# Left-over keys' scores of two pairs as quadrant products, with one tanh and one exp for both

## The chip, the cores and the metric

One core of one Trainium2 chip. The metric is the device time of one execution in microseconds (us), the median of several runs. The instructions of five engines appear below: TensorE (PE; its weight loads are PEld), VectorE (DVE), ScalarE (ACT), GpSimd (POOL) and SyncE (SP), which only starts transfers here. Each engine works through its own queue in order.

## The reference

Attention with a soft cap over 8 batches of 12 heads, 448 positions and 64 dimensions, then a channel mix over the 768 columns of all heads:

```python
scores = scale * q @ k.T                    # per head, 448 x 448
scores = cap * tanh(scores / cap)
attn = exp(scores - max); attn /= attn.sum(-1) + 1e-9
x = attn @ v                                # heads side by side: [8, 448, 768]
x_prev = x shifted by one position
xk = mu_k * x + (1 - mu_k) * x_prev         # xr with mu_r likewise
k = relu(xk @ w_k);  v2 = (k * k) @ w_v     # 768 -> 1024 -> 768
out = sigmoid(xr @ w_r) * v2
```

All tensors are float32.

## The kernel before, in words

The 96 heads are 48 pairs. A program of 55 steps runs pair i's scores, tanh and exp in step i, the values' product of pair i-1, the normalisation and mixing of pair i-2, and the cutting of queries and keys of pair i+2. From step 7 on the products of the key weights (xk @ w_k) of the batch that is complete are spread over the steps as well (`kpart`, line 388: 24 products of 448 columns a step, in four parts K). The products with w_v and w_r fill the second half of the program, from about 547 us on, and the change doesn't touch them.

Scores are computed transposed, keys on the partitions. A pair's 448 keys are three groups of 128 (g = 0, 1, 2) and 64 left-over keys (g = 3). Precision comes from cutting each float32 operand into a high and a low part of a faster type and adding three products (high by high, low by high, high by low). The cutting is `qk_high` (line 180) and `qk_low` (line 202), on GpSimd for most pairs, over tiles of 960 columns: 448 queries, 384 keys, and 128 columns in which the left-over keys of the two heads stand beside zeros, so that one product over all 128 rows gives the scores of both heads (`scores`, line 231; its products are line 238).

`tanh` (line 243, the instruction at 246) and `exp` (line 249, instruction at 256) work on both heads' scores of a group, 128x896, or on 128x448 for g = 3. `red` (line 282, instruction at 284) sums exponentials on VectorE; `gather` (288), `recip` (292), `rec_store` and `rec_load` carry the sums through memory and bring back their reciprocals. `values` (line 258) multiplies uncut float32: line 267 for the groups, and line 277 for the left-over keys of an even and the following odd pair together, in the step behind the odd pair (from pair 6 on; before that, for each pair by itself). In line 277 each product uses 64 rows and 64 columns of the array, one of its four quadrants.

`norm` (line 316, instruction at 317) scales the values' sums; `mix_old` (ScalarE, 327) writes over their accumulator; `mix_new` (VectorE, 332) reads it and releases it. The accumulators `pv` have two buffers, the scores' accumulators `s` have two buffers of two banks. `x_high` and `x_low` (GpSimd, helper lines 93 and 103) cut xk. `gate_old` (GpSimd, 350) and `gate_new` (VectorE, 344) mix for the gate, from pair 12 on.

The order of every queue is written out by hand, as strings of operations that `step` (line 734) walks through. `STEP` serves steps 14 and on (`STEP_2` every sixth of them), `STEP_6` steps 7 to 13, `STEP_7` step 6, `STEP_0` steps 0 to 5. In them S0 to S3 are the scores of the groups, V the values' product, K a part of the key weights' products, and each f one of five VectorE operations that rebuild float32 from the float64 weights (`weight_round`, line 461; in steps up to 42). GpSimd adds their result at line 491 (`weight_sum`). Each engine takes its operations in the order in which they stand there.

Of the kernel before, what the change touches and what calls it, by code (L numbers as in the profile page):

```python
# [13 lines left out]
ALU = mybir.AluOpType  # L14
# [29 lines left out]
KM = 3 * P  # L44
KC = KM + P
LAG = 7
# [20 lines left out]
STEP_6 = """gather load_v x_store weight_load weight_low S0 S1 V S2 f f f f f tanh0 exp0 red0 norm  # L67
weight_sum tanh1 exp1 K relu_early red1 tanh2 qk_rise relu exp2 mix_old k_store mix_new recip rec_store qk_low x_high x_low gate_old
K red2 weight_rest weight_sum relu k_store S3 K K weight_abs tanh3 exp3 red3 gate_new relu k_store load_qk rec_load weight_store"""
STEP_7 = """gather rec_load load_v x_store weight_load weight_low S0 S1 V0 S2 V1 S3 V2 V3 f f f f f tanh0 exp0 red0  # L70
# [8 lines left out]
class Body:  # L79
# [82 lines left out]
    def init_attn(self):  # L162
        self.raw, self.QK, self.rawv, self.S, self.P32, self.PV, self.R, self.rs = ({} for _ in range(8))
        self.tails, self.stored = [], []
# [20 lines left out]
    def qk_first(self):  # L185

        raw = self.raw.pop(0)
# [14 lines left out]
    def qk_low(self, i, e="p"):  # L202
        hi, = self.QK[i]
        lo = self.qp.tile([P, S + KC], F32R, name="qkl")
        self.sub(e, lo, self.raw.pop(i), f(hi))
        self.QK[i] = (hi, lo)

    def row_maxima(self, i):
# [3 lines left out]
        for h in range(2):  # L212
            t = HALF[h]
            for c in range(4):
# [3 lines left out]
                for k, w in ((slice(0, KM), KM), (slice(KM, S), 64)):  # L218
                    first = S + (KM + 64 * ((h + i) % 2) if w == 64 else 0)
# [6 lines left out]
        nc.sync.dma_start(self.max_d.rearrange("h (c p) -> p (h c)", c=4), m)  # L226
        self.M = self.rawp.tile([P, 2, S], F32, name="M", bufs=1)
        for h in range(2):
            nc.sync.dma_start(self.M[:, h], self.max_d[h:h + 1, :].to_broadcast([P, S]))

    def scores(self, i, g):
        nc, qk = self.nc, self.QK[i]
        s = self.ps_s.tile([P, 2, 512], F32, name="s")
        k = slice(S + g * P, S + (g + 1) * P)

        for n, (a, b) in enumerate(((0, 0), (1, 0), (0, 1))):
            for h, p in enumerate(HALF) if g < 3 else [(0, slice(0, P))]:
                nc.tensor.matmul(s[:, (h + i) % 2 if g < 3 else 0, 0:S], qk[a][p, k], qk[b][p, 0:S], start=(n == 0), stop=(n == 2))  # L238
        if g == 3:
            self.QK.pop(i)  # L240
        self.S[i, g] = s

    def tanh(self, i, g):
        n = 2 if g < 3 else 1
        p32 = self.p32p.tile([P, n, S], F32, name=f"p32_{n}", bufs=5 if g < 3 else 3)
        self.nc.scalar.activation(p32, self.S.pop((i, g))[:, :n, 0:S], AF.Tanh, scale=self.scl_t)  # L246
        self.P32[i, g] = p32

    def exp(self, i, g):
        p32 = self.P32[i, g]  # L250
        if self.maxima:
            for h in range(2):
                p, c = (slice(0, P), (h + i) % 2) if g < 3 else (HALF[(h + i) % 2], 0)
                self.nc.vector.scalar_tensor_tensor(out=p32[p, c, :], in0=p32[p, c, :], scalar=self.cap_t[p],
                                                    in1=self.M[p, h, :], op0=ALU.mult, op1=ALU.subtract)
        self.nc.scalar.activation(p32, p32, AF.Exp, scale=1.0 if self.maxima else self.cap_t)  # L256

    def values(self, i, part=None):
# [475 lines left out]
    def step(self, i, KS):  # L734

        nk = nq = 0
        if self.maxima and i < NPAIR:
            self.row_maxima(i)
# [4 lines left out]
        for op in (STEP_0 if i < 6 else STEP_7 if i == 6 else STEP_6 if i < REST[0] else STEP_2 if i % NP == 2 else STEP).split():  # L743
            j = pair.get(op)
# [180 lines left out]
def _layout(inputs):  # L925
# [5 lines left out]
    kt = inputs["k"].reshape(B, NP, 2, S, D).swapaxes(3, 4)  # L931
    qk[..., S:S + KM] = kt[..., :KM]
    v[..., :3, :, :] = vp[:, :, :, :KM].reshape(B, NP, 2, 3, 2, 64, D).transpose(0, 1, 4, 5, 3, 2, 6)
    for h in range(2):
        for odd in range(2):
            t = (h + odd) % 2
            qk[:, odd::2, h, :, S + KM + 64 * t:S + KM + 64 * t + 64] = kt[:, odd::2, h, :, KM:]
            v[:, odd::2, t, :, 3, h] = vp[:, odd::2, h, KM:]
# [26 lines left out]
```

## Time and profile before

| | us |
|---|---|
| median of 3 runs | 913.62 |
| lowest and highest | 912.69, 914.09 |
| span of the profiled execution | 910.9 |
| profiled execution's own time | not listed apart; the runs above lie 1.8 to 3.2 above the span |
| TensorE busy | 889.0 (98%) |
| VectorE, ScalarE, GpSimd busy | 710.2, 642.4, 401.5 |

The profile is one execution, recorded by the hardware. The span runs from the first to the last instruction. An engine's busy time counts its instructions but not their waits. TensorE's matmuls overlap, so one lasts longer than the distance to the next; the cost of one is the distance between starts. A float32 product that isn't cut shows as two instructions, so the values' products of three groups and two heads are "x12". In the chain of waits each piece is the time from its start to the start of the next piece.

### The profile page before, as it was taken

Reading aid. Unit: us, or ns where it says so; the run is one execution under the profiler, and the core shown is the slowest. Engines: PE = TensorE matmul, PEld = TensorE weight load, DVE = VectorE, ACT = ScalarE, POOL = GpSimd, SP = SyncE. Lnnn points to the kernel's source line nnn. Section 1 sums busy time; section 2 is a strip of 40 time slices with the busy share of each in tenths; the row PEclk is TensorE's granted clock in tenths of the full one; section 3 lists DMA queues with packets and bytes.
Section 4 is the critical chain, followed back from the end, with each engine's and each line's share of the span. In section 5 each row is a group of like instructions: output and inputs, shape, how many; then the busy total and the mean of one; then the engine's idle time right before and its main releaser. Section 6 shows DMA issues by size and latency. Waiting matters only on the chain.

```text
span 910.9 us, 15135 instructions
## 1 busy us (share of the span) xinstructions
PE 889.0 (98%) x4986; PEld 713.7 (78%) x4986; DVE 710.2 (78%) x1246; ACT 642.4 (71%) x950; POOL 401.5 (44%) x342
## 2 busy tenths in 40 slices
PE   7879999999999999999999999999999999999996
PEld 3336666667766666766666789999999999999996
DVE  6989976888887888888867766778878767777775
ACT  8998888888878888888877575566565535555553
POOL 5996554777666666776664200000000014444330
PEclk8999999999999999999999999999999999999999
DMA  5565555666666656666565465745454546677663
GB/s 174 163 214 197 187 166 186 203 210 186 208 201 208 204 187 207 206 199 205 163 223 170 128 237 159 240 156 176 143 162 154 180 141 189 217 219 221 215 219 111
DMA packets 123673, 171.61 MB, mean 188 GB/s; under 512 B 22592, under 2 KB 107712, under 8 KB 123584
## 3 DMA queue, kind: packets, MB, share of 16 engines
q1 hardware_dynamic: 114224, 155.67, 54.7%
q10 hardware_dynamic: 9360, 14.88, 4.4%
q8 instruction: 41, 0.67, 0.3%
q14 instruction: 48, 0.39, 0.2%
HBM read 111.48 MB, written 56.60 MB: 185 GB/s over the span
## 4 chain that ended last, share of the span: by engine, by line
PE 87%; DMA 4%; DVE 3%; ACT 2%; SPq 2%; issue 1%; ACTq 0%; DVEq 0%
PE ps L609 39%; PE kps L406 23%; PE s L238 12%; PE pv L267 11%; DMA r<-rec_d 2%; PE pv L277 2%; DMA rec_d<-rs 1%; SPq L290 1%; DVE r L284 1%; ACT p L246 1%; DVE x L317 1%; SPq L313 1%; ACT wvh L724 1%; ACT p L256 0%; DVE xk L332 0%
## 5 line engine op out<-in xcount | busy, mean ns | idle before, releaser
L284 DVE TRANSPOSE_TENSOR_REDUCE r<-p 128x28 f32<-128x896 f32 x192 | 183.5, 979 | 20.1 <-ACT p L256 18.8
L246 ACT ACTIVATE p<-s,scl_t 128x896 f32<-128x896 f32 x192 | 173.2, 902 | 27.8 <-PE s L238 23.9
L256 ACT ACTIVATE p<-p,cap_t 128x896 f32<-128x896 f32 x192 | 182.1, 948 | 6.0 <-ACT pv L327 1.2
L406 PE MATMUL kps<-xkh,wkh 128*128 128x448 f32 x372 | 140.5, 378 | 0.5 <-ACT ko L413 0.5
L406 PE MATMUL kps<-xkl,wkh 128*128 128x448 f32 x372 | 136.0, 365 | 0.0
L406 PE MATMUL kps<-xkh,wkl 128*128 128x448 f32 x372 | 135.9, 365 | 0.0
L573 POOL TENSOR_TENSOR s<-src 128x384 f32<-128x384 f32 x14 | 14.3, 1021 | 265.0 <-DVE lo L594 265.0
L267 PE MATMUL pv<-p,rv 128*64 128x448 f32 x576 | 124.6, 561 | 6.6 <-DVE xk L332 6.6
L609 PE MATMUL ps<-wvh,hi 128*128 128x384 f32 x392 | 131.0, 334 | 0.0
L609 PE MATMUL ps<-wvl,hi 128*128 128x384 f32 x392 | 131.0, 334 | 0.0
L593 ACT CAST hi<-s 128x512 fp32r<-128x512 f32 (+1 forms) x112 | 63.6, 568 | 89.3 <-PE ps L609 76.9
L594 DVE TENSOR_TENSOR lo<-s,hi 128x512 fp32r<-128x512 f32 (+1 forms) x112 | 70.8, 632 | 58.8 <-ACT hi L593 43.7
L103 POOL TENSOR_TENSOR qkl<-rqk,qkh 128x960 fp32r<-128x960 f32 x47 | 106.8, 2273 | 9.9 <-ACT qkh L97 6.6
L609 PE MATMUL ps<-wrh,hi 128*128 128x384 f32 x294 | 98.6, 335 | 0.3 <-DVE o L632 0.3
L609 PE MATMUL ps<-wrl,hi 128*128 128x384 f32 x294 | 98.5, 335 | 0.0
L491 POOL TENSOR_TENSOR wsq<-wa,wsq 128x384 f32<-128x384 f32 (+1 forms) x40 | 44.0, 1100 | 110.7 <-DVE wsq L484 77.1
L593 ACT CAST hi<-src 128x512 fp32r<-128x512 f32 (+1 forms) x84 | 47.6, 567 | 62.3 <-PE ps L609 59.4
L238 PE MATMUL s<-qkh 64*128 64x448 f32 (+1 forms) x336 | 83.5, 439 | 7.8 <-ACT qkh L97 4.1
L238 PEld LDWEIGHTS s<-qkh 64*128 64x128 f32 (+1 forms) x336 | 36.8, 188 | 68.7 <-issue 27.5
L267 PEld LDWEIGHTS pv<-p,rv 128*64 128x64 f32 x576 | 36.4, 138 | 65.3 <-issue 56.2
L406 PEld LDWEIGHTS kps<-xkh,wkh 128*128 128x128 f32 x372 | 69.8, 188 | 20.3 <-issue 13.8
L609 PE MATMUL ps<-wvh,lo 128*128 128x384 f32 x392 | 83.7, 334 | 0.0
(109 smaller groups left out, 1812.8 us busy)
## 6 DMA issues: line engine op xcount, KB each, us to landing
rqk<-qk SPq DMA_DIRECT2D x47, 480.0 KB
k_d<-ko ACTq DMA_DIRECT2D x64, 224.0 KB
src<-k_d SPq DMA_DIRECT2D x56, 256.0 KB
rv<-v SPq DMA_DIRECT2D x48, 256.0 KB
r<-rec_d SPq DMA_DIRECT2D x96, 112.0 KB
v_d<-o SPq DMA_DIRECT2D x56, 192.0 KB
src<-x_d SPq DMA_DIRECT2D x42, 256.0 KB
vl<-v_d SPq DMA_DIRECT2D x56, 192.0 KB
```

The source lines that it names most:

```text
L103: {"p": self.nc.gpsimd, "v": self.nc.vector}[e].tensor_sub(*a)
L238: nc.tensor.matmul(s[:, (h + i) % 2 if g < 3 else 0, 0:S], qk[a][p, k], qk[b][p, 0:S], start=(n == 0), stop=(n == 2))
L246: self.nc.scalar.activation(p32, self.S.pop((i, g))[:, :n, 0:S], AF.Tanh, scale=self.scl_t)
L256: self.nc.scalar.activation(p32, p32, AF.Exp, scale=1.0 if self.maxima else self.cap_t)
L267: nc.tensor.matmul(pv[p, 0:S], v[:, g, h, :], ph[:, (h + i) % 2, :], start=(g == 0), stop=False)
L277: nc.tensor.matmul(self.PV[j][p, 0:S], v[t, 3, h, :], ph[t, 0, :], start=False, stop=True)
L284: self.nc.vector.tensor_reduce(out=r1[:, 0:RM].rearrange("p (x g) -> p x g", g=3)[:, :, g] if g < 3 else r1[:, RM:RC], in_=p32.rearrange(" ...
L406: nc.tensor.matmul(self.kps[fc][:, 0:S], w, m[:, dc, :], start=first, stop=last)
L491: {"p": self.nc.gpsimd, "v": self.nc.vector}[e].tensor_add(sq, f(a), sq)
L593: self.nc.scalar.copy(hi, x)
L594: self.nc.vector.tensor_sub(lo, x, f(hi))
L609: self.nc.tensor.matmul(o, a[:, c, :], w[:, c, :], start=first and k == 0, stop=last and k == len(todo) - 1, skip_group_check=True)
```

## The change

The left-over keys are no longer cut or packed beside zeros: a pair's tile has 896 columns (448 queries, 448 keys). Their scores are computed for an even pair and the following odd one together, in the even pair's step, from the raw float32 tiles: four products, one for each pair and head, each in one quadrant of the array, into the two banks of one `s` tile. In steps 8 and on S3 stands directly behind V, whose last products are quadrants too in even steps. One tanh and one exp over 128x896 serve both pairs. The sums stay separate: `red3` of an odd pair runs at the head of its own step, behind the five weight operations. The raw tiles live longer, so they have three buffers instead of two. The step strings become pairs, for even and odd steps. The scratch size for transfers started by GpSimd, of which there are none, goes to 256. The branch for `maxima` does not run with this input.

```diff
-KC = KM + P
+KC = S
...
-STEP = """gather load_v quad_load x_store weight_load S0 S1 V S2 f f f f f tanh0 exp0 red0
+ODD = """gather load_v quad_load x_store weight_load S0 S1 V S2 f f f f f red3 tanh0 exp0 red0
 weight_sum tanh1 exp1 red1 norm recip rec_store K qk_high qk_low tanh2 relu mix_old k_store prep mix_new x_high x_low gate_old
-K exp2 red2 weight_rest weight_sum relu k_store prep S3 K prep K tanh3 exp3 red3 gate_new relu k_store prep
+K exp2 red2 weight_rest weight_sum relu k_store prep K prep K gate_new relu k_store prep
 weight_abs load_qk rec_load quad_load tail_open weight_store"""
-STEP_2 = STEP.replace("K qk_high", "K S3 qk_high").replace("prep S3 K", "prep K")
-STEP_0 = """gather rec_load load_v x_store weight_load S0 S1 V0 S2 V1 S3 V2 V3 f f f f f tanh0 exp0 red0
-weight_sum tanh1 exp1 weight_abs red1 recip rec_store qk_high qk_low tanh2 exp2 norm red2 tanh3 exp3 mix_old red3 mix_new x_high x_low
+EVEN = ODD.replace("V S2", "V S3 S2").replace(" red3", "").replace("tanh2", "tanh3 tanh2").replace("K gate_new", "K exp3 red3 gate_new")
+ODD_0 = """gather rec_load load_v x_store weight_load S0 S1 V0 S2 V1 V2 V3 f f f f f red3 tanh0 exp0 red0
+weight_sum tanh1 exp1 weight_abs red1 recip rec_store qk_high qk_low tanh2 exp2 norm red2 mix_old mix_new x_high x_low
 load_qk weight_store"""
+EVEN_0 = ODD_0.replace("V1", "V1 S3").replace(" red3", "").replace("red2", "red2 tanh3 exp3").replace("mix_new", "red3 mix_new")
...
     def load_qk(self, i):
-        t = self.raw[i] = self.rawp.tile([P, S + KC], F32, name="rqk")
+        t = self.raw[i] = self.rawp.tile([P, S + KC], F32, name="rqk", bufs=3)
...
     def scores(self, i, g):
-        nc, qk = self.nc, self.QK[i]
-        s = self.ps_s.tile([P, 2, 512], F32, name="s")
+        nc = self.nc
+        s = self.S[i, g] = self.ps_s.tile([P, 2, 512], F32, name="s")
+        if g == 3:
+            for j in (i, i + 1):
+                raw = self.raw.pop(j)
+                for h, p in enumerate(HALF):
+                    nc.tensor.matmul(s[HALF[(h + j) % 2], j % 2, 0:S], raw[p, S + KM:S + KC], raw[p, 0:S], start=True, stop=True)
+            return
+        qk = self.QK[i]
...
     def tanh(self, i, g):
-        n = 2 if g < 3 else 1
-        p32 = self.p32p.tile([P, n, S], F32, name=f"p32_{n}", bufs=5 if g < 3 else 3)
-        self.nc.scalar.activation(p32, self.S.pop((i, g))[:, :n, 0:S], AF.Tanh, scale=self.scl_t)
-        self.P32[i, g] = p32
+        p32 = self.p32p.tile([P, 2, S], F32, name="p32" if g < 3 else "p3", bufs=5 if g < 3 else 2)
+        self.nc.scalar.activation(p32, self.S.pop((i, g))[:, :, 0:S], AF.Tanh, scale=self.scl_t)
+        self.P32[i, g] = p32
+        if g == 3:
+            self.P32[i + 1, g] = p32
...
-                    nc.tensor.matmul(self.PV[j][p, 0:S], v[t, 3, h, :], ph[t, 0, :], start=False, stop=True)
+                    nc.tensor.matmul(self.PV[j][p, 0:S], v[t, 3, h, :], ph[t, j % 2, :], start=False, stop=True)
...
         p32, r1 = self.P32[i, g], self.r1[i % 2]
+        if g == 3:
+            p32 = p32[:, i % 2:i % 2 + 1]
...
-    nc = _bacc.Bacc("TRN2", target_bir_lowering=False, num_devices=1)
+    nc = _bacc.Bacc("TRN2", target_bir_lowering=False, num_devices=1, dynamic_dma_scratch_size=256)
```

`STEP_6` becomes `ODD_6` and `EVEN_6` in the same way: red3 of the odd step behind its f's, S3 behind V in the even step, tanh3 ahead of tanh2, exp3 and red3 behind weight_abs.

## Rows read from the trace of the kernel before

**Rows 1.** Busy time by engine in two windows: window, length, each engine, granted clock, DMA share, GB/s

```profile
28.00:38.00 10.00, 8.24 (x37) 3.01 (x37) 9.12 (x18) 9.80 (x13) 9.44 (x9) 0.83 0.58 176
112.00:505.00 393.00, 393.00 (x2226) 269.44 (x2227) 313.31 (x553) 322.75 (x410) 254.82 (x209) 1.00 0.62 196
```

**Rows 2.** Chain of waits, 155 to 180 us, one early and one late piece: start, length, what

```profile
by line: PE kps L406 41.0%; PE pv L267 28.9%; PE s L238 28.2%; PE pv L277 3.7%
...
155.83 2.41 PE pv L267 x12
...
161.70 0.61 PE s L238 x3
...
166.19 2.41 PE pv L267 x12
168.60 0.91 PE pv L277 x8
...
177.46 2.41 PE pv L267 x12
...
20.37 0.90 PE pv L277 x4
...
457.72 2.41 PE pv L267 x12
```

**Rows 3.** VectorE in order of time: start, length, operation, idle before and releaser

```profile
152.18 0.63 DVE L332 SCALAR_TENSOR_TENSOR xk<-x,mu_k,pv 128x448 f32<-128x448 f32 x1
...
305.49 0.65 DVE L284 TRANSPOSE_TENSOR_REDUCE r<-p 128x14 f32<-128x448 f32 x1 [0.89 <-ACT p L256]
306.90 0.69 DVE L344 SCALAR_TENSOR_TENSOR xg<-x,mu_r,xg 128x448 f32<-128x448 f32 x1 [0.77 <-POOL xg L350]
...
309.75 2.10 DVE L284 TRANSPOSE_TENSOR_REDUCE r<-p 128x28 f32<-128x896 f32 x2
...
313.67 0.63 DVE L332 SCALAR_TENSOR_TENSOR xk<-x,mu_k,pv 128x448 f32<-128x448 f32 x1
...
317.63 0.69 DVE L344 SCALAR_TENSOR_TENSOR xg<-x,mu_r,xg 128x448 f32<-128x448 f32 x1 [1.73 <-POOL xg L350]
```

**Rows 4.** GpSimd in order of time, the same step

```profile
311.98 2.27 POOL L103 TENSOR_TENSOR qkl<-rqk,qkh 128x960 fp32r<-128x960 f32 x1
314.39 0.57 POOL L93 TENSOR_SCALAR xkh<-xk 128x448 fp32r<-128x448 f32 x1
...
316.18 1.42 POOL L350 TENSOR_SCALAR xg<-x,om_r 128x448 f32<-128x448 f32 x1
```

**Rows 5.** TensorE in order of time, after two early idle times

```profile
31.36 1.18 PE L267 MATMUL pv<-p,rv 128*64 128x448 f32 x4 [1.30 <-DVE xk L332]
...
35.52 0.47 PE L238 MATMUL s<-qkh 128*128 128x448 f32 x1
...
40.30 0.97 PE L267 MATMUL pv<-p,rv 128*64 128x448 f32 x4 [0.69 <-DVE xk L332]
...
42.91 0.47 PE L238 MATMUL s<-qkh 128*128 128x448 f32 x1
```

**Rows 6.** Groups by line and shape: exp and tanh on ScalarE

```profile
L256 ACT ACTIVATE p<-p,cap_t 128x896 f32<-128x896 f32 x144 | 149.9, 1041 | 4.5 <-ACT pv L327 1.2
L246 ACT ACTIVATE p<-s,scl_t 128x896 f32<-128x896 f32 x144 | 143.5, 997 | 25.3 <-PE s L238 23.9 <-ACT ko L413 0.8
...
L256 ACT ACTIVATE p<-p,cap_t 128x448 f32<-128x448 f32 x48 | 32.2, 671 | 1.6
...
L246 ACT ACTIVATE p<-s,scl_t 128x448 f32<-128x448 f32 x48 | 29.6, 618 | 2.4 <-ACT ko L413 2.4
```

**Rows 7.** Waits from 111 to 505 us: total, times, longest

```profile
ACT pv L327 <- DVE x L317: 24.5, 27, 1.9
```

**Rows 8.** Chain of waits before 110 us, two pieces

```profile
12.00 0.53 ACT p L246
...
39.08 0.60 DVE r L284
```

More of the change, by code (lines that the diff above doesn't have):

```diff
@@ L52 @@
 LATE = [*range(12), NPAIR - 2, NPAIR - 1]
-STEP = """gather load_v quad_load x_store weight_load S0 S1 V S2 f f f f f tanh0 exp0 red0
+ODD = """gather load_v quad_load x_store weight_load S0 S1 V S2 f f f f f red3 tanh0 exp0 red0
 weight_sum tanh1 exp1 red1 norm recip rec_store K qk_high qk_low tanh2 relu mix_old k_store prep mix_new x_high x_low gate_old
-K exp2 red2 weight_rest weight_sum relu k_store prep S3 K prep K tanh3 exp3 red3 gate_new relu k_store prep
+K exp2 red2 weight_rest weight_sum relu k_store prep K prep K gate_new relu k_store prep
 weight_abs load_qk rec_load quad_load tail_open weight_store"""
-STEP_2 = STEP.replace("K qk_high", "K S3 qk_high").replace("prep S3 K", "prep K")
-STEP_0 = """gather rec_load load_v x_store weight_load S0 S1 V0 S2 V1 S3 V2 V3 f f f f f tanh0 exp0 red0
-weight_sum tanh1 exp1 weight_abs red1 recip rec_store qk_high qk_low tanh2 exp2 norm red2 tanh3 exp3 mix_old red3 mix_new x_high x_low
+EVEN = ODD.replace("V S2", "V S3 S2").replace(" red3", "").replace("tanh2", "tanh3 tanh2").replace("K gate_new", "K exp3 red3 gate_new")
+ODD_0 = """gather rec_load load_v x_store weight_load S0 S1 V0 S2 V1 V2 V3 f f f f f red3 tanh0 exp0 red0
+weight_sum tanh1 exp1 weight_abs red1 recip rec_store qk_high qk_low tanh2 exp2 norm red2 mix_old mix_new x_high x_low
 load_qk weight_store"""
-STEP_6 = """gather load_v x_store weight_load weight_low S0 S1 V S2 f f f f f tanh0 exp0 red0 norm
+EVEN_0 = ODD_0.replace("V1", "V1 S3").replace(" red3", "").replace("red2", "red2 tanh3 exp3").replace("mix_new", "red3 mix_new")
+ODD_6 = """gather load_v x_store weight_load weight_low S0 S1 V S2 f f f f f red3 tanh0 exp0 red0 norm
 weight_sum tanh1 exp1 K relu_early red1 tanh2 qk_rise relu exp2 mix_old k_store mix_new recip rec_store qk_low x_high x_low gate_old
-K red2 weight_rest weight_sum relu k_store S3 K K weight_abs tanh3 exp3 red3 gate_new relu k_store load_qk rec_load weight_store"""
+K red2 weight_rest weight_sum relu k_store K K weight_abs gate_new relu k_store load_qk rec_load weight_store"""
+EVEN_6 = ODD_6.replace("V S2", "V S3 S2").replace(" red3", "").replace("tanh2", "tanh3 tanh2").replace("weight_abs", "weight_abs exp3 red3")
 STEP_7 = """gather rec_load load_v x_store weight_load weight_low S0 S1 V0 S2 V1 S3 V2 V3 f f f f f tanh0 exp0 red0
@@ L162, in init_attn @@
     def init_attn(self):
-        self.raw, self.QK, self.rawv, self.S, self.P32, self.PV, self.R, self.rs = ({} for _ in range(8))
+        self.raw, self.QK, self.rawv, self.S, self.P32, self.PV, self.R, self.rs, self.M = ({} for _ in range(9))
         self.tails, self.stored = [], []
     def load_qk(self, i):
-        t = self.raw[i] = self.rawp.tile([P, S + KC], F32, name="rqk")
+        t = self.raw[i] = self.rawp.tile([P, S + KC], F32, name="rqk", bufs=3)
         self.load_part(i, slice(0, S + (KC if i else P)))
@@ L185, in qk_first @@
     def qk_first(self):
-        raw = self.raw.pop(0)
+        raw = self.raw[0]
         hi, lo = self.QK[0] = [self.qp.tile([P, S + KC], F32R, name=n) for n in ("qkh", "qkl")]
@@ L204, in qk_low @@
         lo = self.qp.tile([P, S + KC], F32R, name="qkl")
-        self.sub(e, lo, self.raw.pop(i), f(hi))
+        self.sub(e, lo, self.raw[i], f(hi))
         self.QK[i] = (hi, lo)
@@ L218, in row_maxima @@
                 for k, w in ((slice(0, KM), KM), (slice(KM, S), 64)):
-                    first = S + (KM + 64 * ((h + i) % 2) if w == 64 else 0)
+                    first = S + k.start
                     for n, (a, b) in enumerate(((0, 0), (1, 0), (0, 1))):
@@ L251, in exp @@
         if self.maxima:
-            for h in range(2):
-                p, c = (slice(0, P), (h + i) % 2) if g < 3 else (HALF[(h + i) % 2], 0)
+            for j, h in [(i, 0), (i, 1)] + [(i + 1, 0), (i + 1, 1)] * (g == 3):
+                p, c = (slice(0, P), (h + i) % 2) if g < 3 else (HALF[(h + j) % 2], j % 2)
                 self.nc.vector.scalar_tensor_tensor(out=p32[p, c, :], in0=p32[p, c, :], scalar=self.cap_t[p],
-                                                    in1=self.M[p, h, :], op0=ALU.mult, op1=ALU.subtract)
+                                                    in1=self.M[j][p, h, :], op0=ALU.mult, op1=ALU.subtract)
         self.nc.scalar.activation(p32, p32, AF.Exp, scale=1.0 if self.maxima else self.cap_t)
@@ L736, in step @@
         nk = nq = 0
-        if self.maxima and i < NPAIR:
-            self.row_maxima(i)
+        if self.maxima and i < NPAIR and i % 2 == 0:
+            for j in (i, i + 1):
+                self.row_maxima(j)
         pair = dict(load_qk=i + 3, qk_high=i + 2, qk_low=i + 2, qk_rise=i + 2, load_v=i, S=i, tanh=i, exp=i, red=i)
@@ L742, in step @@
         pair["x_store"] = i - 3
-        for op in (STEP_0 if i < 6 else STEP_7 if i == 6 else STEP_6 if i < REST[0] else STEP_2 if i % NP == 2 else STEP).split():
+        for op in ((EVEN_0, ODD_0) if i < 6 else (STEP_7,) if i == 6 else (EVEN_6, ODD_6) if i < REST[0] else (EVEN, ODD))[i % 2].split():
             j = pair.get(op)
@@ L931, in _layout @@
     kt = inputs["k"].reshape(B, NP, 2, S, D).swapaxes(3, 4)
-    qk[..., S:S + KM] = kt[..., :KM]
+    qk[..., S:] = kt
     v[..., :3, :, :] = vp[:, :, :, :KM].reshape(B, NP, 2, 3, 2, 64, D).transpose(0, 1, 4, 5, 3, 2, 6)
@@ L936, in _layout @@
             t = (h + odd) % 2
-            qk[:, odd::2, h, :, S + KM + 64 * t:S + KM + 64 * t + 64] = kt[:, odd::2, h, :, KM:]
             v[:, odd::2, t, :, 3, h] = vp[:, odd::2, h, KM:]
```

14 lines of the change are left out of this document (7 added, 7 removed).

## The prediction, made before the change was built

> **What bounds the kernel now.** I read the windows first, then the chain of waits, then each engine's order in time. From 112 to 505 us, most of the attention stage, TensorE is busy in every microsecond while VectorE, ScalarE and GpSimd are busy for 313, 323 and 255 of the 393 us [rows 1]. The chain of waits agrees: from 155 to 180 us it never leaves TensorE [rows 2]. So a step there costs the sum of its products. The values' first product starts at 155.83 in step 15 and at 457.72 in step 43; that is 301.9 us for 28 steps, 21.56 for two. The odd step shown takes 10.36 and the even one 11.27, on average a little less, because the last keys' value products of two pairs stand in the even one (0.91, against 0.61 for the scores of one pair's left-over keys) [rows 2].
>
> A share of 80% says little about a queue that runs in order, so I looked for a loop in VectorE's and GpSimd's orders. There is one. gate_new starts at 306.90 and 317.63, 10.73 apart, and nothing in between waits for TensorE [rows 3]: gate_new and the five weight operations take 2.85 (to 309.75), red0, red1, norm and recip 3.92 (to 313.67), mix_new and the hand-over 0.72, GpSimd's x_high, x_low and gate_old 3.24 (from 314.39) [rows 3, 4]. GpSimd isn't what binds there: qk_low ends at 314.25, mix_new at 314.30, x_high starts at 314.39 [rows 3, 4]. This loop of 10.73 a step stands beside TensorE's 10.78. The small reduction red3 costs nothing in it today: it runs at 305.49, after VectorE has waited 0.89 for it, and 0.77 of waiting for GpSimd follows [rows 3].
>
> The loop reaches TensorE through V, the values' product: its accumulator has two buffers, and V of a step needs mix_new of the step before. Early on V waits for exactly that (1.30 at 31.36) [rows 5]. At step 15 mix_new ended at 152.81, 3.0 us ahead of V [rows 2, 3].
>
> **The change, part by part.**
>
> *Scores of the left-over keys.* Two steps lose 2 x 0.61 = 1.22 [rows 2]. They gain four quadrant products. Their price isn't in the trace; the nearest rows are the values' quadrant products, 0.91 for two pairs with a change of array layout ahead, and a third of the 2.41 that three layers of uncut float32 products take, 0.80 [rows 2]. The new ones follow products of their own layout, so I take 0.80 and keep 0.91 as the other end. TensorE saves 0.42 in two steps, 0.21 a step: 21.14 for two, an odd step 9.7, an even one 11.4.
>
> Do the four really run side by side? One pair's value quadrants (two row halves of the array, one accumulator bank) take 0.90 and two pairs' take 0.91 [rows 2], so neither the halves nor the pairs wait for each other. The Trainium skill (TensorEngine Tiling (Array Packing), "Gotcha 1: PSUM Pressure") says that different row tiles cannot access one PSUM bank at the same time. Here each pair's two halves write one bank, so by that rule the new scores would take 1.6, not 0.80; the trace speaks against it with the 0.90.
>
> *One tanh and exp for two pairs.* ScalarE drops 2 x (0.618 + 0.671) and gains 0.997 + 1.041: 0.54 less in two steps, but 0.75 more in the even one [rows 6]. From 112 us on that is off the path. tanh3 now stands ahead of tanh2, so mix_old, queued behind, comes up to 1.0 later; it waits for norm by 0.9 on average anyway (24.5 us in 27 waits) [rows 7]. Were ScalarE late all the same, mix_new would come later by as much, at most the 1.0. exp3 no longer has tanh3 just ahead of it, so the even step's red3 isn't later than now.
>
> *red3 of odd pairs.* It moves from the slack ahead of gate_new to the place behind the five weight operations, ahead of red0. There it is inside the loop: red0, red1, norm, recip and mix_new queue behind it, then GpSimd, then gate_new. It never waits (its data is a step old) but it costs its length: 0.65 alone, half of a large one (2.10 / 2 / 2 = 0.53) at least [rows 3]. I take 0.55. The loop becomes 10.73 in even steps and 11.28 in odd ones: 22.0 for two, against TensorE's new 21.14.
>
> *Cuts.* 64 of 960 columns leave qk_high and qk_low: some 0.15 off 2.27 [rows 4], hidden, since x_high waits for mix_new; each load of queries and keys shrinks by the same 64 columns, and nothing on the path waits for one. The third buffer for raw keys, the second accumulator of the row maxima's branch and the DMA scratch size move no instruction that runs here; SP's order is unchanged. SP's gather for odd pairs can go after red2.
>
> **The sum**, against the profiled span of 910.9 (its own total isn't listed; the three runs lie 1.8 to 3.2 above the span, the median 2.7, and I keep that distance).
> - Steps 0 to 6: the chain goes through ScalarE in step 0 (tanh3 at 12.00), later norm, red2, red3, gather, the sums' load, norm again [rows 8]. Odd steps lose red3 from it (0.60, steps 3 and 5), the first two steps 0.54 of ScalarE: -1.75. If ScalarE's heavier even step takes its place: 0; with a shorter wait ahead of red2: -2.5.
> - 68 to 112 us: chains through several engines; 0, give or take 1.
> - 112 to 155: four steps at -0.21: -0.85.
> - Steps 15 to 42: TensorE alone would save 28 x 0.21 = 5.9. Its lead of 3.0 falls by 0.86 in two steps: V of step 16 has 1.45 left (3.0 + 9.7 - 11.28), step 18 0.6, step 20 waits 0.25, and the eleven even steps 22 to 42 wait 0.86 each, 9.7 in all. Net +3.8.
> - Steps 43 to 47: no weight operations, the loop is over 2 us shorter and catches up: -1.05. Behind that: 0.
>
> Together -1.75 - 0.85 + 3.8 - 1.05 = +0.15: 913.8 us, no difference that this kernel's measurement (about 0.2%, 1.8 us) can tell.
>
> The new waits of 0.86 could lower TensorE's clock. From 28 to 38 us the granted clock is 0.83 on average, so part of it was at 1.2 GHz and not at 2.4 [rows 1]: after an idle 1.30 there the next products took 4.16 (31.36 to 35.52), while after an idle 0.69 the same products took 2.61 (40.30 to 42.91) [rows 5]. A fall would cost 1.55 in one step, but the loop doesn't wait for TensorE, so the waits behind it would shrink by as much; under 1 us would remain.
>
> **The rivals.**
> *TensorE stays the bound.* Then every step from 112 to 505 saves 0.21: 36.5 x 0.21 = 7.7, with 1.75 early 9.4: 904.4 us. It needs room in the loop that I don't see: a VectorE wait between the weight operations and mix_new into which red3 falls. For it: the lead of 3.0 is never used up today. Against: at 309.75 the reductions follow the weight operations with no wait [rows 3].
> *The row halves wait for each other* (slower). The change then doesn't do what it says: the new scores take 1.6 on TensorE in each even step, more than the 1.22 they replace. Two steps take 21.94, the loop's 22.0 hardly binds, and 0.38 more for each two of 36.5 steps is +6.9; less 1.75: 918.8 us. It decides from about 1.3 us for four products. The 0.90 of one pair's quadrants speaks against it; for it, only that scores and values differ in their source.
>
> **How the numbers follow.** The loop case gets 0.62, TensorE as the bound 0.25, serial halves 0.13. Inside the loop case the early gain (0 to -2.5), red3's length (0.53 to 0.65, eleven times), the quadrants' 0.80 to 0.91 and 68 to 112 us give 911 to 917.5; I split it 0.18 faster, 0.26 the same, 0.18 slower by over 0.2%. With the rivals: faster 0.43, same 0.26, slower 0.31. The range reaches down past the first rival, 903.5, and up to 917.5; it leaves out the second.
>
> **What the new profile would show.** Right: in the even steps from about 20 to 42, V waits 0.8 to 0.9 for mix_new (some 10 us in all); gate_new's spacing alternates between 10.7 and 11.3; the four new products take 0.8. Wrong: no such waits and 21.1 for two steps (the first rival), or 1.6 for the products (the second). Also wrong: gate_new still 10.7 apart after odd steps, or VectorE waiting ahead of red0 for exp0.

## The result and the profile after

The changed kernel takes 919.71 us (median of 4 runs, 917.79 to 923.07) against 913.15 us (912.53 to 914.09) beside it: 1.0078 times the time before, 95% interval 1.0056 to 1.0101. It is slower by some 6 us. The forecast was 913.8, with a range that ended at 917.5.

The profiled execution has a span of 920.9 us, 10.0 more than before; with 923.07 it is the slowest of the four, so the split below shows some 3 us more than the medians do. The marks of the split stand in both traces: the values' first product in steps 15 and 43, norm of step 48 (the last but one), the first product of the stage that follows the attention, and the end of the span. Differences are taken before rounding.

| from, to | before | after | difference | forecast |
|---|---|---|---|---|
| start, values of step 15 | 155.8 | 158.0 | +2.1 | -2.6 |
| step 15, step 43 | 301.9 | 304.7 | +2.8 | +3.8 |
| step 43, norm of step 48 | 57.8 | 58.2 | +0.5 | -1.05 |
| norm of 48, next stage | 31.4 | 34.5 | +3.1 | 0 |
| next stage, end | 364.0 | 365.5 | +1.5 | 0 |

The loop in the 28 steps in the middle came out as the forecast's theory had it. First VectorE in the order of time (start, length, operation, idle before it and releaser), one odd and one even step, to be held against [rows 3]:

```profile
307.78 0.63 DVE L343 SCALAR_TENSOR_TENSOR xk<-x,mu_k,pv 128x448 f32<-128x448 f32 x1
...
311.72 0.69 DVE L355 SCALAR_TENSOR_TENSOR xg<-x,mu_r,xg 128x448 f32<-128x448 f32 x1 [1.04 <-POOL xg L361]
...
314.57 2.63 DVE L295 TRANSPOSE_TENSOR_REDUCE r<-p 128x14 f32<-128x448 f32 x3
...
319.01 0.62 DVE L343 SCALAR_TENSOR_TENSOR xk<-x,mu_k,pv 128x448 f32<-128x448 f32 x1
...
322.95 0.68 DVE L355 SCALAR_TENSOR_TENSOR xg<-x,mu_r,xg 128x448 f32<-128x448 f32 x1 [2.29 <-POOL xg L361]
```

gate_new (line 355) to gate_new is 11.23 us here, 10.73 in [rows 3]; the next spacing is 10.71 again, and so in turn. The three reductions red3, red0, red1 take 2.63, where two took 2.10: red3 costs 0.53 in the loop. GpSimd, in the same step, now waits for VectorE where it had work up to that point in [rows 4]:

```profile
319.72 0.57 POOL L95 TENSOR_SCALAR xkh<-xk 128x448 fp32r<-128x448 f32 x1 [0.84 <-DVE xk L343]
...
321.51 1.41 POOL L361 TENSOR_SCALAR xg<-x,om_r 128x448 f32<-128x448 f32 x1
```

And TensorE waits for mix_new in the even step, then runs the values' products (276, 286) and the four new score products (240):

```profile
319.69 2.48 PE L276 MATMUL pv<-p,rv 128*64 128x448 f32 x12 [0.63 <-DVE xk L343]
322.09 0.98 PE L286 MATMUL pv<-p,rv 64*64 64x448 f32 x8
322.90 0.93 PE L240 MATMUL s<-rqk 64*64 64x448 f32 x8
323.76 0.47 PE L247 MATMUL s<-qkh 64*128 64x448 f32 x2
```

The eight instructions of the four score products start in two groups of four, the four of a group within 0.02 us and the groups 0.38 apart (322.90 to 322.92, 323.27 to 323.29), so the four run side by side. From start to next start they take 0.86 here. In the chain of waits, where lengths run to the next piece, they take 0.75 in an earlier step and stand beside two pairs' value quadrants at 0.91 as in [rows 2]:

```profile
80.58 0.91 PE pv L286 x8
81.49 0.75 PE s L240 x8
82.24 0.80 PE s L247 x6
```

The waits from 112 to 505 us (total, times, longest) hold the new one, which the kernel before didn't have, 8 times on the products and 10 times on the weight loads ahead of them; ScalarE's wait for norm, 24.5 us in [rows 7], has doubled:

```profile
ACT pv L338 <- DVE x L328: 53.0, 31, 2.6
...
PEld pv L276 <- DVE xk L343: 8.7, 10, 1.4
...
PE pv L276 <- DVE xk L343: 4.9, 8, 1.0
```

The granted clock didn't fall with these waits: 1.00 over the whole stretch, as in [rows 1], with TensorE busy for 385 of 393 us, so idle for 7.5:

```profile
112.00:505.00 393.00, 385.46 (x2254) 254.07 (x2252) 308.59 (x554) 305.90 (x372) 246.12 (x208) 1.00 0.63 192
```

One wait the forecast doesn't have. In steps 14, 20, 26, 32, 38 and 44 the products of the key weights (K, line 417) stop for ScalarE's copy of the finished ones (`ko`, 424). Step 14, in TensorE's order:

```profile
152.08 0.37 PE L417 MATMUL kps<-xkl,wkh 128*128 128x448 f32 x1
152.71 0.47 PE L417 MATMUL kps<-xkh,wkh 128*128 128x448 f32 x1 [0.26 <-ACT ko L424]
```

From start to start that is 0.63 where 0.20 is usual, 0.43 lost. The kernel before had the left-over scores at this very place in these steps, by `STEP_2`, which the change dropped:

```profile
149.73 0.36 PE L406 MATMUL kps<-xkl,wkh 128*128 128x448 f32 x1
149.93 0.36 PE L238 MATMUL s<-qkh 128*128 128x448 f32 x1
```

And ScalarE comes to the copy later, since both tanh3 and tanh2 stand ahead of it now. All ten profiles of the changed kernel and its variants have this wait in these six steps, none of the six profiles of the kernel before and its variants has it.

How late VectorE gets shows in gate_new of steps 42 and 47, before

```profile
457.68 0.68 DVE L344 SCALAR_TENSOR_TENSOR xg<-x,mu_r,xg 128x448 f32<-128x448 f32 x1 [1.73 <-POOL xg L350]
...
511.20 0.68 DVE L344 SCALAR_TENSOR_TENSOR xg<-x,mu_r,xg 128x448 f32<-128x448 f32 x1 [1.71 <-POOL xg L350]
```

and after:

```profile
465.19 0.69 DVE L355 SCALAR_TENSOR_TENSOR xg<-x,mu_r,xg 128x448 f32<-128x448 f32 x1 [1.76 <-POOL xg L361]
...
516.58 0.68 DVE L355 SCALAR_TENSOR_TENSOR xg<-x,mu_r,xg 128x448 f32<-128x448 f32 x1 [2.26 <-POOL xg L361]
```

It is 7.5 us later in step 42 and 5.4 in step 47 (1.6 in step 14). TensorE, at step 43, is 5.0 later.

The end is what the forecast had at nothing. The chain of waits before (start, length, what), from norm of step 48 on:

```profile
515.48 0.54 DVE x L317
...
517.42 2.04 DMA rec_d<-rs
...
532.01 14.86 PE kps L406 x72
546.87 13.18 PE ps L609 x76
```

and after:

```profile
520.86 0.54 DVE x L328
...
522.78 3.65 DMA rec_d<-rs
...
538.94 16.42 PE kps L417 x72
555.36 4.71 PE ps L620 x27
```

Norm is 5.4 us later, the small store of the reciprocals lands in 3.65 instead of 2.04, and the last 72 key products take 16.42 instead of 14.86. From the last norm to these products it is 9.0 us in both. So in both kernels the attention stage ends with a chain norm, store, load, norm, and TensorE's last products wait for it. The 16.42 belongs to this execution: over these products the granted clock is 0.90, so part of them ran at 1.2 GHz and not at 2.4; in the second profile (e_after) it is 1.00, and they take 15.13.

### The profile page after: what moved, and what is told of

It is laid out like the page before. It is cut to its first block, busy times and chain, and to the rows that moved or that the text cites. A ratio compares the mean times of both kernels' runs of the same rounds, so it can differ in the third digit from the quotient of the medians.

```text
span 920.9 us, 15166 instructions
## 1 busy us (share of the span) xinstructions
PE 883.2 (96%) x5034; PEld 696.1 (76%) x5034; DVE 706.5 (77%) x1246; ACT 625.6 (68%) x902; POOL 391.9 (43%) x342
## 4 chain that ended last, share of the span: by engine, by line
PE 49%; DVE 15%; DMA 15%; SPq 7%; ACT 6%; issue 4%; POOL 3%; DVEq 0%; ACTq 0%; POOLq 0%
PE ps L620 38%; DMA sq__194<-r 7%; PE kps L417 5%; DVE r L295 4%; SPq L301 4%; DMA rec_d<-rs 4%; PE pv L276 2%; SPq L324 2%; ACT p L265 2%; DVE x L328 2%; DMA r<-rec_d 2%; ACT p L253 2%; PE s L247 2%; DVE sq__194 L305 2%; DMA rqk<-qk 2%
## 5 line engine op out<-in xcount | busy, mean ns | idle before, releaser
L295 DVE TRANSPOSE_TENSOR_REDUCE r<-p 128x28 f32<-128x896 f32 (+1 forms) x192 | 181.0, 972 | 17.2 <-ACT p L265 17.1
L265 ACT ACTIVATE p<-p,cap_t 128x896 f32<-128x896 f32 x168 | 173.7, 1040 | 11.0 <-DMA x_d<-xg 2.9
L253 ACT ACTIVATE p<-s,scl_t 128x896 f32<-128x896 f32 x168 | 165.2, 996 | 17.7 <-PE s L247 9.9
L105 POOL TENSOR_TENSOR qkl<-rqk,qkh 128x896 fp32r<-128x896 f32 x47 | 99.7, 2122 | 10.6 <-ACT qkh L99 7.4
L338 ACT ACTIVATE pv<-x,om_k 128x448 f32<-128x448 f32 x48 | 30.6, 639 | 70.2 <-DVE x L328 70.1
L247 PEld LDWEIGHTS s<-qkh 64*128 64x128 f32 x288 | 27.9, 189 | 64.7 <-ACT p L253 24.7
```

Source lines behind the costliest of these rows:

```text
L105: {"p": self.nc.gpsimd, "v": self.nc.vector}[e].tensor_sub(*a)
L247: nc.tensor.matmul(s[:, (h + i) % 2, 0:S], qk[a][p, k], qk[b][p, 0:S], start=(n == 0), stop=(n == 2))
L253: self.nc.scalar.activation(p32, self.S.pop((i, g))[:, :, 0:S], AF.Tanh, scale=self.scl_t)
```

## The experiments

Each ran beside the kernel before on one chip; ratios are to that. "15" and "43" are the starts of the values' first product in these steps in the one profiled execution, so a span need not lie where the median lies. All moves of order hold from step 14 on unless a run says otherwise.

| run | 15 | 43 | 28 steps | span | median | ratio and interval |
|---|---|---|---|---|---|---|
| e_before | 154.5 | 456.3 | 301.9 | 910.1 | 913.26 | 1.0004 (0.9993 to 1.0014) |
| e_after | 157.0 | 461.8 | 304.8 | 918.7 | 918.61 | 1.0052 (1.0033 to 1.0072) |
| e_red3 | 155.6 | 454.3 | 298.7 | 909.5 | 914.05 | 1.0000 (0.9986 to 1.0015) |
| e_gate | 155.7 | 456.5 | 300.8 | 912.9 | 912.18 | 0.9991 (0.9975 to 1.0006) |
| e_gate_before | 155.2 | 457.0 | 301.9 | 913.5 | 914.09 | 1.0010 (0.9997 to 1.0022) |
| e_ramp | 157.9 | 463.4 | 305.6 | 922.5 | 919.51 | 1.0059 (1.0045 to 1.0074) |
| e_end | 155.4 | 459.9 | 304.5 | 917.5 | 921.15 | 1.0083 (1.0070 to 1.0096) |
| e_open | 156.8 | 461.9 | 305.2 | 919.4 | 924.31 | 1.0119 (1.0103 to 1.0136) |
| e_open_before | 154.8 | 464.1 | 309.4 | 921.0 | 924.11 | 1.0117 (1.0101 to 1.0133) |
| e_xg2 | 156.3 | 454.0 | 297.7 | 907.8 | 908.88 | 0.9946 (0.9930 to 0.9961) |
| e_xg2_red3 | 156.2 | 453.8 | 297.6 | 907.3 | 909.11 | 0.9951 (0.9935 to 0.9966) |
| e_early | 159.0 | 463.4 | 304.4 | 920.3 | 922.72 | 1.0104 (1.0086 to 1.0122) |
| e_before_raw3 | 156.2 | 458.1 | 301.9 | 911.0 | 912.89 | 0.9997 (0.9988 to 1.0006) |
| e_xg2_before | 157.4 | 459.3 | 301.9 | 912.2 | 911.89 | 0.9991 (0.9979 to 1.0003) |

### Both kernels once more (e_after, e_before)

> The changed kernel once more, beside the three below on the same chip, to see how far its time and its profile repeat. Theory (the loop of VectorE and GpSimd sets the pace, its lag lasts to the end of the attention stage): gate_new's spacing alternates between 10.7 and 11.2 again, V of step 43 comes some 304.7 us behind V of step 15, and the last norm lies some 5 to 7 us later than in the kernel before. Rival (the loss is the memory transfers' scatter in one execution): the median lies near 913 and the last norm within 2 us of the kernel before.

> The kernel before, unchanged, for a second profile: values' product of step 15 at 155 to 156 us, stage 301.9, step 43 at 457 to 458, from there to the end of the span 453 to 454.5, total 913 to 914.

Both repeat within 0.2 us in the middle. The start scatters by 1 to 1.5 us from execution to execution, so the +2.1 of one profile says little. The second pair of profiles has the same lag of gate_new: 8.1 us in step 42 and 6.3 in step 47 (1.9 in step 14).

### red3 taken out of the loop again (e_red3)

```diff
-... V S2 f f f f f red3 tanh0 exp0 red0
+... V S2 f f f f f tanh0 exp0 red0
-... prep K prep K gate_new relu k_store prep
+... prep K prep K red3 gate_new relu k_store prep
```

The even steps keep their order.

> Only red3 of the odd pairs goes back to the place ahead of gate_new, from step 14 on; scores, tanh and exp of the left-over keys stay as changed. Theory (red3 inside the loop is what lengthens it): gate_new 10.7 apart in every step, V of step 43 some 297 to 301 us behind V of step 15 and not 304.7, total some 4 to 7 us below the changed kernel, 913 to 916. Rival (the even step's heavier ScalarE or the new products set the pace): the stage and the total stay within 1 us of the changed kernel.

The 28 steps fall by 6.1 us, and the spacing of gate_new is 10.7 in odd and even steps alike. So the place of red3 is what held the changed kernel there: 0.53 in each odd step. gate_new's lag behind the kernel before is gone as well: against e_before 0.6 us in step 14 and 0.1 in step 42. The median falls from 918.61 to 914.05, which is 4.6 of the 5.5 us that the changed kernel lost beside it (913.09 before). But the stage ends at the loop's 10.7, not at TensorE's pace, and the total is only that of the kernel before.

### The loop shortened on GpSimd (e_gate, e_gate_before)

```diff
-... prep mix_new x_high x_low gate_old
+... prep mix_new gate_old x_high x_low
```

> The changed kernel with gate_old ahead of x_high and x_low on GpSimd from step 14 on, so that gate_new no longer waits for the two cuts: the loop is opened. Theory: no wait of V for mix_new in steps 16 to 42, TensorE sets the pace at 21.1 us for two steps, V of step 43 some 295 to 297 us behind V of step 15, total 908 to 912, below the kernel before. Rival (TensorE itself got slower by the quadrant products or by its clock): 21.5 or more for two steps and a total above 914.

> The kernel before with the same reordering on GpSimd and nothing of the change. Theory (there TensorE sets the pace and the loop only stands beside it): V of step 43 still 301.5 to 302 us behind V of step 15, total within 1 us of 913.2. Rival (the loop already held the kernel before back): 3 us faster or more.

gate_new now waits for gate_old alone. The changed kernel gains 4.0 us in the 28 steps, half of what was expected; the kernel before gains nothing there, as its bound is TensorE. The other half met a new wait in e_gate, in the waits from 156 to 457 us:

```profile
POOL xg L361 <- DMA x_d<-xg: 21.0, 17, 2.4
```

gate_old writes xg, which has one buffer, and comes so early now that the step before's xg is still being stored. A second cost shows on GpSimd and on VectorE in one step:

```profile
230.40 1.41 POOL L361 TENSOR_SCALAR xg<-x,om_r 128x448 f32<-128x448 f32 x1 [0.59 <-DMA x_d<-xg]
...
232.42 1.38 POOL L105 TENSOR_TENSOR xkl<-xk,xkh 128x448 fp32r<-128x448 f32 x1
```

```profile
231.84 0.96 DVE L355 SCALAR_TENSOR_TENSOR xg<-x,mu_r,xg 128x448 f32<-128x448 f32 x1
232.73 1.29 DVE L486 TENSOR_SCALAR wsq<-wsq 128x384 f32<-128x384 f32 x1
```

The first weight operation (486) takes 1.29 where it took 0.35 in the changed kernel at 312.32 us; it ends 0.22 after x_low does (234.02, 233.80). The Trainium skill (SBUF — State Buffer, "Who interferes with whom") has a rule for this: VectorE and GpSimd share one pair of ports, a tensor_scalar of VectorE can run in a mode that takes this pair, and then the engine that issued first holds it for the whole instruction while the other is blocked. The trace agrees, with 1.29 instead of 0.35 and the end 0.22 behind x_low's; that the operation ran in this mode no row shows.

### The same with a second buffer for xg (e_xg2, e_xg2_red3, e_xg2_before)

```diff
-            self.xg = self.up.tile([P, S], F32, name="xg", bufs=1)
+            self.xg = self.up.tile([P, S], F32, name="xg", bufs=2)
```

> The run named e_gate (the changed kernel with gate_old ahead of x_high and x_low from step 14 on) and a second buffer for xg, so that gate_old needn't wait until the step before's xg has been stored. Theory (after that wait is gone the loop through VectorE and GpSimd is some 2.5 us shorter than TensorE's step): the waits of GpSimd for the store vanish, the 28 steps from 15 to 43 take 296.5 to 298.5 us (e_gate: 300.8; the changed kernel: 304.8), the total is 908 to 911. Rival (a second loop stands beside it, through SP: recip, rec_store, its landing, rec_load, gather, its landing, recip, of 10 to 11 us with landings that vary): stage 299 to 301, total 911 to 913.5.

> The changed kernel with gate_old ahead of x_high and x_low, two buffers for xg and red3 of odd pairs back ahead of gate_new (steps from 14 on). Theory: nothing is left of the loop through GpSimd, the even steps gain another 0.55 of VectorE; stage 296 to 297.5, total 907 to 910. Rival (the loop through SP): 298 to 300, total 910 to 914.

> The kernel before with the two moves of the run named e_xg2 (gate_old ahead of x_high and x_low from step 14 on, two buffers for xg): what of that run's gain is the change's, and what the moves'? Theory (before is bound by TensorE from 112 us on, so that a shorter loop gives nothing there): stage 301.9, total 912.5 to 914; then the whole gain of e_xg2 against before is the products that the change saves. Rival: the moves gain by themselves, total under 911.

With the wait for the store gone the 28 steps take 297.7, mix_new ends 1.0 to 3.6 us ahead of each values' product there, and the total is 908.88: faster than both kernels. The two V that bound the 28 steps of e_xg2, in TensorE's order:

```profile
156.34 2.48 PE L276 MATMUL pv<-p,rv 128*64 128x448 f32 x12
...
454.00 2.48 PE L276 MATMUL pv<-p,rv 128*64 128x448 f32 x12
```

Taking red3 out as well adds nothing (909.11): once the loop is short enough, the place of red3 is free. The kernel before with the same two moves stays at 911.89, 28 steps at exactly 301.9. So of the gain of e_xg2 the moves alone have at most 0.2%, and the rest, 0.9946 against 0.9991 or about 4.1 us, is the change's own products, set free: 301.9 - 297.7 = 4.2 in the profiles. That is what the change, as built, was worth on TensorE in these steps.

### The loop shortened on VectorE (e_open, e_open_before)

```diff
-... weight_load S0 S1 V S2 f f f f f red3 tanh0 exp0 red0
+... weight_load weight_store S0 S1 V S2 red3 tanh0 exp0 red0
-K exp2 red2 weight_rest weight_sum ...
+K exp2 red2 f f f f f weight_rest weight_sum ...
-weight_abs load_qk rec_load quad_load tail_open weight_store
+weight_abs load_qk rec_load quad_load tail_open
```

> The changed kernel with the five weight operations of VectorE moved in the steps from 14 on from ahead of the reductions to behind red2, where VectorE stands idle for 2.3 us until GpSimd has made xg; the store of the weights moves to the next step's loads, so that SP's queue doesn't wait for it. Theory (the loop through VectorE and GpSimd is what holds the changed kernel; the weight operations are 2.85 of its 10.7): the loop falls under TensorE's 10.6 a step, values' products wait for mix_new nowhere by more than 0.3, the 28 steps from 15 to 43 take 296 to 298 us instead of 304.8, and with the four subtractions of step 48 out of the end's chain as well the total is 905 to 909. Rival one (VectorE beside GpSimd runs slower, weight operations of 1.3 instead of 0.57 us): stage 299 to 301, total 909 to 913. Rival two (it is not this loop that holds the even steps): stage 303 to 305, total 916 to 919.

> The kernel before with the same move as the run named e_open. Theory (TensorE is its bound from 112 us on): 28 steps still take 301.9, only the end can gain, by the four subtractions of step 48 that leave its chain: 911 to 914. If the stage falls below 301.5, TensorE was not its bound alone.

Both fell: no gain in the changed kernel's 28 steps, and the kernel before loses 7.5 there. The weight operations left the loop's front and landed beside GpSimd's work. One step of e_open on VectorE:

```profile
274.64 1.14 DVE L486 TENSOR_SCALAR wsq<-wsq 128x384 f32<-128x384 f32 x1
275.82 0.68 DVE L489 TENSOR_SCALAR wa<-wsq 128x384 uint32<-128x384 uint32 x1
```

and GpSimd beside it:

```profile
274.43 1.14 POOL L105 TENSOR_TENSOR xkl<-xk,xkh 128x448 fp32r<-128x448 f32 x1
275.55 1.51 POOL L361 TENSOR_SCALAR xg<-x,om_r 128x448 f32<-128x448 f32 x1
```

VectorE's busy time from 112 to 505 us is 339.5 us, against 308.6 in the changed kernel above. And a second loop came up, in the chain of waits of e_open:

```profile
250.89 4.07 DMA rec_d<-rs
...
255.56 1.09 SPq L324
...
256.74 0.55 SPq L301
...
258.61 1.74 DMA sq__194<-r
...
260.46 0.52 DVE sq__194 L305
```

rec_store must land before SP, in its order, issues rec_load (324) and then gather (301); gather must land before recip (305); recip makes the next rec_store. From recip's end at 250.88 to the next recip's start that is 9.6 us, and mix_new stands behind recip on VectorE. In how many steps this loop and in how many the ports set the pace wasn't separated.

### The start (e_ramp, e_early, e_before_raw3)

```diff
-EVEN_6 = ODD_6....replace("tanh2", "tanh3 tanh2")...
+EVEN_6 = ODD_6....replace("exp2 mix_old", "exp2 mix_old tanh3")...
```

> The changed kernel with one move in the even steps 8, 10 and 12: tanh3 stands behind mix_old instead of ahead of tanh2; nothing else. Theory (in these steps the shared tanh holds up mix_old, so mix_new, recip behind it and rec_store come up to 1.0 us later each time): the values' product of step 15 starts at 155.0 to 156.0 us instead of 156.9 to 158.0, the 28 steps after it still take 304.6 to 304.9, the total falls by 1 to 2 us, to 916.5 to 917.5. Rival (the ramp is late because loads and stores land later by chance, not because of the order on ScalarE): step 15 stays at 157 to 158, total 918 to 919.

In e_early, steps 0 to 13 run one order for odd and even steps again, and tanh and exp of the left-over keys (left out below) take one pair's half there:

```diff
-EVEN_0 = ODD_0....
+EVEN_0 = ODD_0 = ODD_0.replace("V1", "V1 S3").replace(" red3", "").replace("red2", "red2 tanh3 exp3")...
-EVEN_6 = ODD_6....
+EVEN_6 = ODD_6 = ODD_6.replace(" red3", "").replace("k_store K K weight_abs", "k_store S3 K K weight_abs tanh3 exp3 red3")
...
-            for j in (i, i + 1):
+            for j in (i, i + 1) if i >= REST[0] else (i,):
```

> The changed kernel with its steps 0 to 13 undone: there each pair's left-over scores, tanh, exp and red3 stand alone again and in the order of the kernel before (still uncut quadrant products, 0.8 instead of 0.61 on TensorE); steps from 14 on as changed. Theory (the early part of the change costs 1 to 2 us instead of the forecast gain of 2.6, and the loop passes it on): mix_new of step 15 ends at 151.5 to 153 us (changed kernel: 153.3 and 154.4), the values' product of step 43 starts at 459.5 to 461 instead of 461.8 and 462.6, total 917 to 918.5. Rival (the early part is no loss, only landings of transfers scatter): mix_new of step 15 ends at 153 to 154.5, total 918.6 to 920.

```diff
-        t = self.raw[i] = self.rawp.tile([P, S + KC], F32, name="rqk")
+        t = self.raw[i] = self.rawp.tile([P, S + KC], F32, name="rqk", bufs=3)
-... name=f"p32_{n}", bufs=5 if g < 3 else 3)
+... name=f"p32_{n}", bufs=5 if g < 3 else 2)
```

> The kernel before with the change's third buffer for raw queries and keys, and nothing else of it (to make room the left-over keys' probabilities have two buffers instead of three). Theory (the third buffer lets SP issue its first loads 2 us earlier, and that, not the order of tanh, exp and red3, makes the first 70 us of the changed kernel 1 us later): norm of step 2 starts at 29.0 to 29.6 instead of 27.9 to 28.6, the values' product of step 7 at 67.8 to 69 instead of 66.8 to 67.9, total 914 to 915.5. Rival (the buffer costs nothing; the heavier step 0 on ScalarE and VectorE does): 28.0 to 28.6, 66.8 to 67.9, total 913 to 913.8.

None of my three explanations of the start accounts for the time. e_ramp: step 15 stays at 157.9 and the ratio, 1.0059, near e_after's 1.0052, so tanh3 ahead of tanh2 in steps 8 to 12 isn't the cause, as far as this scatter lets one tell. e_early, with the order undone, is at 159.0 and 922.72, no better than the changed kernel. e_before_raw3: SP's load of the third pair's raw keys, the second of the two issues in each line below, does start earlier, in e_before (5.76)

```profile
3.06 3.03 SPq L174 DMA_DIRECT2D rqk<-qk  x2
```

and in e_before_raw3 (3.54)

```profile
3.06 0.91 SPq L174 DMA_DIRECT2D rqk<-qk  x2
```

and two of the three signs that were expected of it are there: the first norm, in step 2, starts at 29.0 us, later than in each of the five profiles with two buffers (27.9 to 28.8), and the values' product of step 7 at 68.5 (which says less: those five spread from 66.8 to 69.8). But the third isn't: the time is 0.9997 of before. What is left is this: with the order and the buffers of before the values' product of step 15 starts at 154.5 to 157.4 in five profiles (155.5 on average), with those of the changed kernel at 155.4 to 158.0 in nine (156.5, e_ramp among them). The forecast gain of 2.6 isn't there; a loss of 1.0 is hardly more than the scatter. From the values' product of step 14 to that of step 15 it is 11.27 us in each of the five and 11.89 in each of the nine, and 0.43 of the difference is the wait of K for ScalarE.

### The end (e_end)

```diff
-... prep mix_new x_high x_low gate_old
+... prep mix_new f_late f_late f_late f_late x_high x_low gate_old
```

Here f_late are the four subtractions of steps 46 and 48, which stand no longer among the f ahead of tanh0.

> The changed kernel with the four large subtractions of steps 46 and 48 (3.6 us of VectorE each) moved from their place ahead of norm to behind mix_new; nothing else. Theory (the end is set by VectorE's lag and the chain norm, recip, rec_store, rec_load, norm, not by TensorE): up to step 43 nothing changes (stage 304.6 to 304.9), the last pair's recip and rec_store come 2 to 3 us earlier, the products of the weights' stage start at 550 to 551.5 us instead of 553.3, total 915.5 to 917. Rival (TensorE's products set the end): these start at 553 to 555 as before, total 918 to 919.

Not the gain expected. In step 48 norm no longer waits for the subtractions, but they come back in front of the last norm, longer now, since GpSimd works beside them:

```profile
521.23 0.94 DVE L729 TENSOR_TENSOR w<-w,w 128x768 f32<-128x768 f32 x1
522.20 1.20 DVE L729 TENSOR_TENSOR wa<-w,w 128x768 f32<-128x768 f32 x1
523.33 1.91 DVE L729 TENSOR_TENSOR w<-w,w 128x768 f32<-128x768 f32 x1
525.16 0.95 DVE L729 TENSOR_TENSOR wsq<-wsq,wa 128x768 f32<-128x768 f32 x1
...
528.63 0.61 DVE L328 TENSOR_TENSOR x<-pv,r 128x448 f32<-128x448 f32 x1
```

The last norm is at 528.6, against 529.3 in e_after, and the next stage starts at 552.4 against 553.3. The ratio of 1.0083 is above e_after's but inside the interval of the first measurement, so the run shows no gain and no loss. That the loop's lag reaches the end shows in another way: from step 43 to the end of the span it is 453.2 and 453.8 us in the two profiles of before, 458.3 and 456.9 in those of the changed kernel, and 453.8 again in e_xg2, where nothing lags. Alone this number proves little: e_gate_before has 456.4 without such a lag, after GpSimd has waited up to 5.2 us there for the store of xg.

## Why the prediction was wrong

The steps that failed are the gain at the start ("-1.75" and part of "-0.85"), "From 112 us on that is off the path", and "Behind that: 0". By the averages of the profiles the start is off by 3.6 us (-2.6 forecast, +1.0 found). The loop with its end is off by 1.9 (3.8 - 1.05 forecast, 4.6 by the median of e_red3).

**Right: the loop.** The place, the size (0.53 against 0.55), the alternation 10.7 and 11.2 and the even steps from the twenties on that wait are confirmed by the traces. e_red3 and e_xg2 take the loop's hold away in two ways, while e_xg2_before and e_gate_before show nothing to take away in the kernel before. That the price of the 28 steps came out near too (+2.8 and +2.9 against +3.8) is in part luck: two terms were too large and nearly cancel. Against e_xg2, which TensorE bounds, the changed kernel loses 7.0 us to the waits and not 9.7, and TensorE saves 4.2 and not 5.9.

**Right: the quadrants run side by side.** 0.75 to 0.86 for four products, which start together. The rule of the Trainium skill that the forecast weighed (TensorEngine Tiling (Array Packing), "Gotcha 1: PSUM Pressure") would have given twice that; the trace is against it here too. A sum by that rule gives 918.8, near the result, and would have been right for a wrong reason: its 0.38 in each two steps isn't in the trace. (The sum of the other rival is 904.2, not 904.4.)

**Wrong: ScalarE's heavier even step, "From 112 us on that is off the path."** In every sixth step it holds up TensorE: K waits for ScalarE's copy, and S3, which hid that wait in `STEP_2`, is gone from there. The four waits of 0.43 in the 28 steps are 1.7 us, which is what TensorE's saving falls short of the forecast (4.2 against 5.9); the one in step 14 takes half of the "-0.85" of 112 to 155 us. No run put S3 or another product back into that place, so this is read from the traces alone.

**Wrong: steps 0 to 6, "-1.75".** The first odd step that lost red3 does get shorter: norm of step 3 to that of step 4 is 7.7 to 8.5 in eight of nine profiles with the changed order (9.1 in e_after), where the five with the order of before have 8.6 to 9.1. But the first norm, at 27.9 to 28.8 in those five, comes at 29.1 to 29.6 in the nine, where "the first two steps 0.54 of ScalarE" should have brought it forward. The heavier step 0, the forecast's bad case, would explain that; but e_early, with step 0 as before, has 29.4 too, and e_before_raw3, with nothing of the change but the third buffer, has 29.0. So the sentence that the third buffer moves "no instruction that runs here" is wrong, and the buffer is what all the late profiles have in common; that it causes the delay rests on one profile without the rest of the change, and its total didn't move. At step 15 no gain is left; how it was lost on the way is open, but for the 0.43 of step 14. The sum took the saving of single operations for that of a chain that passes through transfers, and from execution to execution alone step 15 shifts by up to 3 us.

**Right, but of no use: "Steps 43 to 47: no weight operations, the loop is over 2 us shorter and catches up: -1.05."** gate_new's lag falls from 7.5 to 5.4 us in these steps, and TensorE's from 5.0 in step 43 to 4.0 in step 48. But steps 46 and 48 have four subtractions of 0.95 in the place of the weight operations, 3.8 us where these had 2.85 (gate_new around those of step 46 is 12.06 apart before and 12.03 after), and what the end waits for is norm of step 48, which is 5.4 late.

**Wrong: "Behind that: 0."** It rested on TensorE setting the end, which no row of the forecast showed: none was read behind 505 us. So the sum carried on only what TensorE had lost, while VectorE was later by more: gate_new's lag grows from 1.6 us in step 14 to 7.5 in step 42, and TensorE, which at first has slack towards the loop, feels only part of it. The end hangs on VectorE's chain, and there the lag goes straight on. In the profile 3.1 us come on top, half from the landing of the last reciprocals and half from the key products behind it, at a granted clock of 0.90. The latter is the fall of the clock that the forecast priced at 1.55 in one step, and thought nearly harmless because the loop doesn't wait for TensorE; here nothing hides it, but it came in three of ten profiles only. In the next stage another 1.5 follow, 0.7 of it a wait for VectorE; e_xg2, without the lag, takes as long there, so this part isn't the lag's. Why the last reciprocals land in 3.6 to 4.4 us in six profiles of the changed kernel and its variants, in 2.3 and 2.5 in the two with two buffers for xg, and in about 2 in both of the kernel before, is open.

## What to carry to other kernels

A saving on the bound engine is worth only what the next loop leaves free: look for loops through in-order queues by the spacing of one instruction from step to step, and when one stands within a few per cent of the bound, shorten it in the same change. Follow a lag to the last link of its stage before writing zero behind it, on the engine that has it. Before dropping a special order, find the wait that it hid (`STEP_2`). And when a move lets an operation start earlier, look at what it reuses (the one buffer of xg cost 3.1 of 7.2 us) and at what it now runs beside.

## What the runs showed of the hardware

VectorE and GpSimd hold each other up far more than the kernel before lets one see, since its order keeps them apart: 0.35 became 1.29, and 0.95 became 1.91, beside GpSimd's copies and subtractions. The store of one pair's reciprocals landed in 1.26 us at one place and in 5.46 at another of the same execution (e_after). And short waits of TensorE, at most 1.0 us once in two steps, left its granted clock at 1.00 (112 to 505 us of the changed kernel). Ahead of the last 72 key products TensorE is idle for 2.5 to 3.6 of 9.0 us in the three profiles in which these then take 16.4 to 16.6 us at 0.90 (after, e_gate, e_ramp); in e_after and e_red3 it is idle for 2.9 and 3.2, and they take 15.1 and 14.9 at 1.00.
